# Block-causal attention with a gated linear unit: w_out loaded to all 128 partitions, and a new written order of the work

## The chip, the cores and the metric

The kernel runs on one core of a Trainium2 chip. A core has five engines, each with its own queue of instructions that it runs in order: TensorE (PE: matrix products, with weight loads, PEld, beside them), VectorE (DVE), ScalarE (ACT), GpSimd (POOL) and SyncE (SP, which here issues nearly all transfers). Sixteen DMA engines move the data. The engines wait for each other and for transfers through semaphores. The metric is the time of one execution in microseconds (us).

## The reference

All values are 32 bit floating point. B = 8 batches, H = 8 heads, S = 576 positions, D = 64.

```python
# attention, block-causal in blocks of 64
scores = (1/sqrt(64)) * q @ k^T               # per batch and head, 576 x 576
scores = where(pos_i // 64 >= pos_j // 64, scores, -1e9)
attn = softmax(scores)
x = (attn @ v), heads side by side            # (8, 576, 512)
# gated linear unit with a causal convolution of 5 taps
gate = sigmoid(sum_k conv_w[k] * x shifted by (4 - k) positions)
val = x @ w_val                               # 512 x 512
out = (gate * val) @ w_out                    # 512 x 512
```

## The kernel before

**The work and its names.** The kernel's text holds one long list of words, PLAN; `run` reads it from left to right and calls, for each word, the function that issues that piece of work. Since each engine runs its own instructions in order, the list fixes the order on every engine, and the order of transfers on SP. Nothing else schedules. A word is a name, its indices, and after @ an engine (A = ACT, D = DVE, P = POOL) or the PSUM banks that it uses.

A number Q from 0 to 15 stands for four heads of one batch (Q = 2 x batch + half). For each Q:

- `Lk.Q`, `Lq.Q` load k and q of four heads (576 KB each, line 178) into one of three buffers `qks`.
- `cq.Q.i` casts them to 16 bit (`qk`, line 172, i = 0 for q and 1 for k; the first pair is cast in two pieces), `T.Q.i` transposes on DVE (line 235).
- `s.Q.t` makes score tiles t = 0, 1, 2 on PE; `e.Q.t.a` takes the exponential on ACT (line 269, written into `pt`); `m.Q.t` zeroes the masked corner on POOL (line 285). `sl.b` and `el.b.a` are the last 64 positions of a batch.
- `av.Q.a` multiplies with v, 30 products for two heads; the ones column of v gives the sum, and `n.Q.a` divides by it on DVE (lines 316 and 317) into one of four buffers `x`.

v comes per batch b: `Lv.b.c` loads 128 positions of all heads (256 KB, line 187), c = 0 to 3, `cv.b.0` casts chunks 0 and 1, `cv.b.1` chunks 2 and 3, on POOL. `Lvt.b` and `cvt.b` are the last 64 positions. An `av` of batch b needs all of them.

Then x has to be turned: `xtr.p` (p = 2Q + a, 0 to 31) does it with five products on PE (line 324), followed by a copy `xt.p` out of PSUM on DVE or ACT; or `dx.p` does it as a transposing transfer from SP (line 333), without PE. Before: 13 of the first sort and 19 of the second.

The gated unit works on ten units n: 0 to 7 are the first 512 positions of each batch, 8 and 9 gather the last 64 positions of four batches each (`tt.b` copies them on POOL, line 338). `cn.n` is the convolution (80 small products), `th.n` the gate on ACT (line 366), `val.n.x` the product with w_val (four matrix products), `gv.n.x` gate times value on DVE (line 384), `o.n.t` the product with w_out (four matrix products), `oc.n.t` the copy out of PSUM, `st.n.t` the store (line 416).

**The weights.** w_val comes in two loads (`Lwv`, line 196), and w_out in four (`Lwo.0` to `Lwo.3`, line 201), into buffers `th` that the gates use later. `wo.f@engine` casts half of w_out to 16 bit: f = 0 the columns 0 and 1 of the buffer, f = 1 the columns 2 and 3. Before, `Lwo.j` fills all four columns of 32 partitions, so each `wo` needs all four loads. `w@bank` are products of zeros that keep PE busy while it has nothing to do at the start.

**The first transfers.** `START` issues `Lk.0 Lq.0`; then come the words of PLAN. DVE also builds the convolution's diagonal weights at the start (`cT`, `DG`, lines 428 and 433).

Of the kernel before, what the change touches and what calls it, by code (L numbers as in the profile page):

```python
# [19 lines left out]
el.0.1 s.1.0@0123 e.1.1.1 av.0.0@67 cq.2.1@P e.1.0.0 n.0.0 e.1.0.1 s.1.2@0145 m.1.1 cq.2.0@P T.2.1  # L20
av.0.1@67 e.1.2.1 xtr.0@2 e.1.2.0 m.1.0 T.2.0 cq.3.1@P xt.0@A n.0.1 w@3 w@3 w@3 s.2.1@0145 m.1.2
cq.3.0@P av.1.1@23 e.2.1.0 T.3.1 Lq.4 Lwv.0 e.2.1.1 s.2.2@0167 n.1.1 Lv.1.3 e.2.2.1 av.1.0@45 m.2.1
Lv.1.2 T.3.0 e.2.2.0 s.2.0@2367 n.1.0 cv.1.0@P e.2.0.1 xtr.3@0 xtr.1@1 xt.3@D xtr.2@4 e.2.0.0 m.2.2
xt.1@D xt.2@D w@5 sl.1@0167 cq.4.0@P s.3.0@2345 el.1.1 Lvt.1 el.1.0 e.3.0.0 cn.0@0167 Lk.4 tt.0
wv.0@D Lwo.1 wv.2@P T.4.0 e.3.0.1 Lq.5 val.0.0@2 Lwo.0 wv.3@A wv.1@D Lwo.3 m.2.0 m.3.0 Lk.5
val.0.1@3 th.0.0 cv.1.1@P Lwo.2 Lv.3.1 th.0.1 s.3.2@0145 gv.0.0 Lv.2.0 cvt.1@P gv.0.1 e.3.2.1
av.2.0@67 cq.4.1@P e.3.2.0 av.2.1@23 n.2.0 s.3.1@0145 m.3.2 n.2.1 xtr.4@6 e.3.1.0 val.0.3@7 cq.5.0@P
T.4.1 e.3.1.1 xtr.5@2 val.0.2@3 gv.0.3 xt.4@A m.3.1 xt.5@D s.4.1@0145 gv.0.2 av.3.1@67 e.4.1.1 T.5.0
cq.5.1@P Lv.2.1 e.4.1.0 s.4.2@2345 n.3.1 e.4.2.1 av.3.0@01 Lq.6 wo.0@D wo.1@P Lk.7 e.4.2.0 T.5.1
Lvt.2 s.4.0@4567 Lk.6 m.4.1 n.3.0 xtr.7@2 Lv.2.2 m.4.2 e.4.0.1 o.0.3@3 Lv.2.3 e.4.0.0 xt.7@D  # L30
sl.2@0167 oc.0.3@D cv.2.0@P o.0.1@2 el.2.0 el.2.1 xtr.6@3 m.4.0 oc.0.1@A s.5.2@0145 xt.6@D cq.6.0@P
cn.1@2367 e.5.2.1 e.5.2.0 tt.1 T.6.0 val.1.2@4 cq.7.1@P th.1.1 o.0.2@5 th.1.0 m.5.2 Lv.4.0 gv.1.2
cvt.2@P s.5.0@0167 T.7.1 oc.0.2@A cq.6.1@P val.1.0@4 Lv.3.0 e.5.0.0 val.1.1@5 gv.1.0 e.5.0.1 Lq.7
T.6.1 s.5.1@0123 Lk.8 cv.2.1@P val.1.3@4 Lv.3.3 e.5.1.0 gv.1.1 st.0.3 m.5.0 av.4.0@67 Lk.9 e.5.1.1
gv.1.3 Lv.4.3 s.6.1@0145 n.4.0 m.5.1 cv.3.0@P av.5.0@23 e.6.1.0 xtr.8@6 e.6.1.1 n.5.0 o.1.3@7
cq.7.0@P xt.8@A s.6.2@0145 oc.1.3@D st.0.1 xtr.10@2 m.6.1 e.6.2.0 T.7.0 Lvt.3 o.1.2@3 cq.8.1@P Lvt.4
xt.10@A s.6.0@0167 oc.1.2@D e.6.2.1 o.1.1@2 T.8.1 e.6.0.0 m.6.2 av.5.1@45 oc.1.1@D Lv.5.1 e.6.0.1
av.4.1@01 n.5.1 cq.9.1@P s.7.2@2367 n.4.1 Lq.8 o.1.0@4 e.7.2.0 m.6.0 st.0.2 Lv.4.2 xtr.9@5 e.7.2.1
oc.1.0@D s.7.1@0123 cvt.3@P Lv.3.2 xt.9@D xtr.11@4 cvt.4@P e.7.1.1 o.0.0@5 xt.11@D m.7.2 tt.2
e.7.1.0 sl.3@2367 oc.0.0@D el.3.1 T.9.1 s.7.0@0145 m.7.1 el.3.0 cn.2@2367 e.7.0.0 Lq.9 cq.8.0@P  # L40
Lv.4.1 e.7.0.1 val.2.0@0 Lk.10 T.8.0 th.2.0 Lv.5.0 m.7.0 cv.4.1@P val.2.2@1 th.2.1 gv.2.0 s.8.1@2345
cv.3.1@P val.2.3@0 gv.2.2 e.8.1.1 Lq.11 av.7.0@67 st.1.3 e.8.1.0 gv.2.3 cq.9.0@P st.1.2 s.8.2@0145
Lq.10 n.7.0 Lv.5.3 av.6.1@23 e.8.2.1 cv.4.0@P T.9.0 av.6.0@67 e.8.2.0 m.8.1 Lk.11 n.6.1 cq.10.1@P
dx.14 sl.4@0145 n.6.0 el.4.0 el.4.1 m.8.2 s.9.2@0123 val.2.1@4 T.10.1 e.9.2.0 dx.12 av.7.1@67
cq.11.0@P e.9.2.1 gv.2.1 s.8.0@0145 n.7.1 cv.5.0@P o.2.0@2 e.8.0.1 T.11.0 m.9.2 o.2.2@3 e.8.0.0
dx.15 cq.10.0@P oc.2.0@D s.9.1@4567 Lk.13 oc.2.2@A xtr.13@0 e.9.1.1 o.2.1@1 xt.13@D m.8.0 T.10.0
e.9.1.0 s.9.0@2367 Lv.6.2 oc.2.1@D e.9.0.0 cq.11.1@P av.8.1@45 e.9.0.1 Lv.5.2 s.10.0@0123 n.8.1
m.9.1 e.10.0.0 av.8.0@67 m.9.0 T.11.1 e.10.0.1 s.10.1@0145 tt.3 n.8.0 e.10.1.1 av.9.1@23 m.10.0
dx.17 e.10.1.0 st.2.0 cq.13.1@P cn.3@4567 n.9.1 st.1.1 st.1.0 st.2.1 m.10.1 val.3.3@0 Lq.12 th.3.1
# [44 lines left out]
def kernel(  # L94
# [16 lines left out]
    B, H, SEQ, D = q.shape  # L111
# [24 lines left out]
    DG = const([128, 20, 32], fp16, "DG")  # L136
# [16 lines left out]
    ths = ring(NTH, [128, 4, 512], fp32, "th")  # L153
# [14 lines left out]
    def eng(e, dflt):  # L168
        return ENG[e] if e else dflt
# [340 lines left out]
```

## Time and profile before

| what | value |
|---|---|
| median of 3 runs | 185.18 us (183.21, 185.18, 188.44) |
| the profiled execution's own time | 183.79 us |
| its span, first to last instruction | 182.0 us |
| granted TensorE clock | 0.98 |
| PE busy | 160.2 us (88%) |
| ACT busy | 130.0 us (71%) |
| DVE busy | 116.4 us (64%) |
| POOL busy | 86.8 us (48%) |
| bytes moved by transfers | 43.41 MB |

The span is 1.79 us shorter than the execution's time. Busy times of PE are modelled and include overlap of pipelined products, so that a busy PE is not one at its peak. A transfer's time in the profile runs from its issue on SP to its landing, with the waiting behind earlier transfers in it.

### The profile page before, as it was taken

Reading aid. Unit: us, or ns where it says so; the run is one execution under the profiler, and the core shown is the slowest. Engines: PE = TensorE matmul, PEld = TensorE weight load, DVE = VectorE, ACT = ScalarE, POOL = GpSimd, SP = SyncE. Lnnn points to the kernel's source line nnn. Section 1 sums busy time; section 2 is a strip of 40 time slices with the busy share of each in tenths; the row PEclk is TensorE's granted clock in tenths of the full one; section 3 lists DMA queues with packets and bytes.
Section 4 is the critical chain, followed back from the end, with each engine's and each line's share of the span. In section 5 each row is a group of like instructions: output and inputs, shape, how many; then the busy total and the mean of one; then the engine's idle time right before and its main releaser. Section 6 shows DMA issues by size and latency. Waiting matters only on the chain.

```text
span 182.0 us, 6859 instructions
## 1 busy us (share of the span) xinstructions
PE 160.2 (88%) x2938; PEld 93.0 (51%) x2938; DVE 116.4 (64%) x188; ACT 130.0 (71%) x160; POOL 86.8 (48%) x147
## 2 busy tenths in 40 slices
PE   7796989878798998898998996899999996999991
PEld 2434665636353764485474453655534754755540
DVE  7970897574747798589685438982646874455510
ACT  3499799883789698886995776697899564044461
POOL 6167979542788656877654156645237201000000
PEclk9999699996999999999999999999999999999999
DMA  5999999999999999999999999999999485553155
GB/s 199 370 165 337 383 284 254 266 197 173 247 285 226 305 344 215 303 300 368 205 229 188 385 317 270 296 173 171 222 290 342 136 151 162 107 94 112 69 212 191
DMA packets 61368, 43.41 MB, mean 239 GB/s; under 512 B 51477, under 2 KB 51733, under 8 KB 61338
## 3 DMA queue, kind: packets, MB, share of 16 engines
q1 hardware_dynamic: 61184, 42.84, 96.2%
q8 instruction: 23, 0.38, 0.9%
q10 hardware_dynamic: 154, 0.14, 0.2%
q14 instruction: 7, 0.06, 0.1%
HBM read 30.42 MB, written 9.44 MB: 219 GB/s over the span
## 4 chain that ended last, share of the span: by engine, by line
PE 30%; DMA 28%; SPq 20%; issue 7%; POOL 6%; DVE 4%; ACT 4%; POOLq 0%; DVEq 0%
PE PS L115 29%; DMA qks<-in_k_dram 15%; SPq L187 7%; DMA qks<-in_q_dram 7%; DMA vst<-in_v_dram 5%; SPq L178 4%; SPq L416 3%; POOL qk L172 3%; ACT pt L269 3%; SPq L192 3%; DMA xt<-x 2%; DVE qkT L235 2%; SPq L333 2%; DVE gv L384 1%; POOL w_out L172 1%
## 5 line engine op out<-in xcount | busy, mean ns | idle before, releaser
L269 ACT ACTIVATE pt<-PS 128x1024 f16<-128x1024 f32 x96 | 92.4, 1029 | 22.8 <-PE PS L115 20.1
L172 POOL CAST qk<-qks 128x1152 f16<-128x1152 f32 x30 | 44.6, 1487 | 32.3 <-DMA qks<-in_q_dram 16.5
L235 DVE STREAM_TRANSPOSE qkT<-qk 128x576 f32<-128x576 f32 (+2 forms) x34 | 39.3, 1164 | 12.8 <-POOL qk L172 12.5
L115 PE MATMUL PS<-qkT 32*128 32x64 f16 (+4 forms) x768 | 34.5, 280 | 7.8 <-DVE x L317 2.1
L115 PEld LDWEIGHTS <-pt 128*128 128x128 f16 x960 | 33.9, 100 | 13.5 <-issue 6.2
L115 PE MATMUL PS<-v,pt 128*128 128x65 f16 x896 | 35.8, 198 | 5.7 <-POOL pt L285 2.3
L384 DVE SCALAR_TENSOR_TENSOR gv<-th,PS 128x512 f16<-128x512 f32 (+1 forms) x40 | 26.4, 694 | 16.4 <-ACT th L366 11.5
L115 PE MATMUL PS<-w_out,gv 128*128 128x512 f16 x144 | 34.9, 380 | 0.6 <-POOL w_out L172 0.3
L115 PE MATMUL PS<-xt,w_val 128*128 128x512 f16 x128 | 31.6, 380 | 1.3 <-DMA xt<-x 1.2
L115 PEld LDWEIGHTS <-qkT 32*128 32x128 f16 x768 | 15.7, 94 | 26.6 <-issue 18.6
L366 ACT ACTIVATE th<-PS 128x1024 f32<-128x1024 f32 (+1 forms) x20 | 17.7, 942 | 14.2 <-PE PS L115 14.1
L317 DVE TENSOR_TENSOR x<-PS,rc 128x640 f16<-128x640 f32 x32 | 26.4, 825 | 1.2
L115 PEld LDWEIGHTS <-w_val 128*128 128x128 f16 x160 | 14.2, 97 | 14.7 <-issue 3.4
L115 PEld LDWEIGHTS <-gv 128*128 128x128 f16 x144 | 12.9, 98 | 16.3 <-issue 3.6
L172 POOL CAST v<-vst 128x1024 f16<-128x1024 f32 x16 | 16.6, 1044 | 9.0 <-DMA vst<-in_v_dram 7.9
L285 POOL MEMSET pt<- 64x128 f32 x64 | 11.5, 199 | 15.3 <-ACT pt L269 12.9
L316 DVE RECIPROCAL rc<-PS 128x10 f32<-128x10 f32 x32 | 6.6, 206 | 15.5 <-PE PS L115 13.5
L172 DVE COPY osb<-PS 128x512 f32<-128x512 f32 x17 | 11.5, 682 | 6.2 <-PE PS L115 3.4
L172 ACT COPY osb<-PS 128x512 f32<-128x512 f32 x18 | 10.6, 589 | 4.6 <-PE PS L115 4.4
L115 PE MATMUL PS<-v16t,pt 128*128 128x65 f16 x64 | 12.6, 197 | 0.0
L115 PEld LDWEIGHTS <-DG 32*32 32x32 f16 x800 | 9.0, 88 | 5.3 <-issue 4.0
L115 PE MATMUL PS<-xt,DG 32*32 32x512 f16 x640 | 11.2, 377 | 0.0
(44 smaller groups left out, 71.7 us busy)
## 6 DMA issues: line engine op xcount, KB each, us to landing
qks<-in_k_dram SPq DMA_DIRECT2D x16, 576.0 KB, 6.7
qks<-in_q_dram SPq DMA_DIRECT2D x16, 576.0 KB, 6.4
out_dram<-osb SPq DMA_DIRECT2D x35, 256.0 KB, 4.6
vst<-in_v_dram SPq DMA_DIRECT2D x32, 256.0 KB, 7.1
vtst<-in_v_dram SPq DMA_DIRECT2D x8, 128.0 KB, 6.9
th<-in_moe_w_val_dram SPq DMA_DIRECT2D x2, 512.0 KB, 8.5
th<-in_moe_w_out_dram SPq DMA_DIRECT2D x4, 256.0 KB, 10.4
xt<-x SPq DMA_TRANSPOSE x19, 4.4
```

The source lines that it names most:

```text
L115: nc.tensor.matmul(out=out, lhsT=lhsT, rhs=rhs, start=start, stop=stop, skip_group_check=True)
L172: (e.copy if e is nc.scalar else e.tensor_copy)(out=o, in_=i)
L178: eng(m, nc.sync).dma_start(out=qks[Q % NQS][0:128, i], in_=rows)
L187: eng(m, nc.sync).dma_start(out=vst[b % NVS][0:128, c], in_=v[b, 0:8, 128 * c:128 * c + 128].rearrange("h p d -> p h d"))
L192: eng(m, nc.sync).dma_start(out=vtst[b % 2][0:64, 0:8, 0:64], in_=v[b, 0:8, 512:576].rearrange("h s d -> s h d"))
L235: nc.vector.transpose(out=qkT[Q % NQT][0:128, i].bitcast(fp32)[:, :, 0:288] .rearrange("p a (i n) -> p n a i", n=9)[:, n], in_=qk16[Q % NQ ...
L269: nc.scalar.activation(out=prob(Q, t)[0:128, 2 * a:2 * a + 2, 0:512], in_=PS[0:128, k0:k0 + 2], func=AF.Exp, bias=0.0, scale=0.125)
L285: nc.gpsimd.memset(prob(Q, t)[64:128, 0:4, o:o + 64].bitcast(fp32), 0.0)
L316: nc.vector.reciprocal(out=rc[0:128], in_=O[:, :, :, 64:65])
L317: nc.vector.tensor_tensor(out=x16[p % NX16][0:128].rearrange("p i h d -> p h i d"), in0=O[:, :, :, 0:64], in1=rc[0:128].to_broadcast([128, ...
L366: nc.scalar.activation(out=ths[UO.index(n) % NTH][0:128, 2 * r:2 * r + 2, 0:w], in_=PS[0:128, k0:k0 + 2, 0:w], func=AF.Tanh, bias=0.0, sca ...
L384: nc.vector.scalar_tensor_tensor(out=o, in0=t, scalar=1.0, in1=u, op0=ALU.add, op1=ALU.mult)
```

## The change

Two things change. The first is the load of w_out. A row of w_out has the number 128 x a + 32 x b + i, with a and b from 0 to 3 and i from 0 to 31. Before, load number a took all rows of one a; now load number b takes all rows of one b, for a = 0 to 3 and i = 0 to 31 in this order, and writes them to all 128 partitions, column b of the buffer. Each load still moves 128 rows of 2 KB, and each row ends where it ended before. So a cast `wo.0` needs `Lwo.0` and `Lwo.1` only, `wo.1` the other two.

The second is PLAN: another order of nearly all words and other banks, with the same work except for the following. Four more x tiles are turned on PE and four fewer by a transposing transfer (17 and 15); their copies are five on ACT and twelve on DVE (four and nine before). There is one zero product less (32). The casts of weights go to other engines: `wo.0` on POOL and `wo.1` on ACT (DVE and POOL before), three of the four `wv` on DVE and one on POOL (two on DVE, one each on POOL and ACT before). One piece of the first cast of q goes to POOL instead of DVE, and one copy of an output from ACT to DVE.

```diff
     def load_w_out(j, m):
         eng(m, nc.sync).dma_start(
-            out=ths[1][32 * j:32 * j + 32],
-            in_=moe_w_out[128 * j:128 * j + 128].rearrange("(x i) n -> i x n", x=4))
+            out=ths[1][0:128, j],
+            in_=moe_w_out.rearrange("(j x i) n -> x j i n", j=4, x=4)[j])
```

The order of the transfers on SP up to the loads of w_out, of batch 3's v and of the last q and k (the other words between them left out; "..." marks left out transfers):

```diff
-Lcw Lk.1 Lq.1 Lv.0.1 Lvt.0 Lv.0.0 Lv.0.2 Lv.0.3 Lk.2 Lq.2 Lk.3 Lq.3 Lwv.1 Lv.1.1 Lv.1.0 Lq.4 Lwv.0
-Lv.1.3 Lv.1.2 Lvt.1 Lk.4 Lwo.1 Lq.5 Lwo.0 Lwo.3 Lk.5 Lwo.2 Lv.3.1 Lv.2.0 Lv.2.1 Lq.6 Lk.7 Lvt.2 Lk.6
-Lv.2.2 Lv.2.3 Lv.4.0 Lv.3.0 Lq.7 Lk.8 Lv.3.3 st.0.3 Lk.9 Lv.4.3 st.0.1 Lvt.3 Lvt.4 Lv.5.1 Lq.8 st.0.2
-Lv.4.2 Lv.3.2
...
-dx.22 dx.23 dx.20 Lv.7.2 Lv.6.1 st.3.2 st.3.1 st.8.0 Lq.15 st.3.3 Lk.15 st.3.0 Lvt.6
+Lcw Lq.1 Lk.2 Lk.1 Lq.2 Lv.0.0 Lv.0.2 Lv.0.3 Lvt.0 Lv.0.1 Lk.4 Lq.3 Lk.3 Lq.4 Lk.5 Lv.1.0 Lv.1.1
+Lwv.1 Lwv.0 Lv.1.2 Lv.1.3 Lvt.1 Lwo.0 Lq.5 Lwo.3 Lv.2.2 Lv.2.0 Lwo.1 Lwo.2 Lq.7 Lk.8 Lk.6 Lq.6 Lk.7
+Lv.2.3 Lv.2.1 Lvt.2 Lv.3.0 Lq.8 Lv.3.2 st.0.1 Lv.3.1 Lvt.3 Lvt.4 Lk.9 Lk.10 Lv.4.1 Lv.3.3
...
+dx.16 st.8.0 st.3.0 Lvt.6 st.8.1 dx.18 Lv.6.0 dx.19 st.3.2 st.2.0 Lv.6.1 Lv.7.1 Lk.15 Lq.15 Lvt.7
```

The order on PE around the first use of batch 3's v and from the first use of batch 6's v to the end (banks left out):

```diff
-s.7.0 cn.2 val.2.0 val.2.2 s.8.1 val.2.3 av.7.0 s.8.2 av.6.1 av.6.0 sl.4 s.9.2 val.2.1 av.7.1
...
-av.12.1 s.15.2 av.12.0 o.5.3 av.13.0 sl.7 av.13.1 s.15.1 o.5.1 o.5.0 s.15.0 av.14.1 av.14.0 val.6.3
-av.15.1 av.15.0 val.6.1 cn.6 val.6.0 val.6.2 o.5.2 val.7.1 val.9.0 val.9.3 cn.9 o.6.3 o.6.0 val.9.2
-val.9.1 val.7.2 cn.7 o.6.2 val.7.3 val.7.0 o.9.0 o.6.1 o.7.0 o.7.3 o.7.2 o.7.1 o.9.1
+s.7.2 av.5.0 s.6.0 xtr.11 xtr.10 sl.3 o.1.2 s.8.0 av.7.1 av.7.0 av.6.0 s.8.1 xtr.14 val.2.2
...
+av.12.0 s.13.0 o.4.2 val.5.1 cn.5 val.5.3 val.5.0 val.5.2 sl.7 av.12.1 s.13.2 o.5.0 o.5.1 s.15.0 o.4.0
+av.13.0 s.15.1 av.13.1 s.15.2 o.5.3 s.14.2 o.5.2 av.15.0 av.15.1 av.14.1 av.14.0 val.6.3 val.6.0 xtr.28
+cn.6 val.6.1 val.6.2 val.7.2 val.9.2 val.9.0 cn.9 o.6.3 val.9.1 val.9.3 o.6.0 cn.7 val.7.3 val.7.0
+val.7.1 o.6.2 o.9.0 o.6.1 o.7.1 o.7.2 o.7.3 o.7.0 o.9.1
```

The head of the list, where DVE's `DG` (1.90 us) moves ahead of the transposes `T.0.0`:

```diff
-w@7 cw@0 T.0.1.1 T.0.1.0 cq.0.0.0@A cq.0.0.1@D cT T.0.0.1 T.0.0.0 cq.1.1@P DG w@4 w@4 w@4 w@4 w@4
+w@7 w@7 cw@0 T.0.1.1 T.0.1.0 cT DG cq.0.0.0@A cq.0.0.1@P T.0.0.1 cq.1.0@P T.0.0.0 w@4 w@4 w@4 w@4
```

More of the change, by code (lines that the diff above doesn't have):

```diff
@@ L20 @@
[L20 to L25, printed above, removed]
@@ new lines @@
+xtr.28@0 cn.6@4567 xt.28@A val.6.1@0 th.6.0 val.6.2@1 th.6.1 gv.6.0 tt.7 val.7.2@4 gv.6.1 gv.6.3
+val.9.2@0 gv.6.2 val.9.0@5 cn.9@2367 o.6.3@1 th.9.0 th.9.1 gv.9.0 val.9.1@2 oc.6.3@A val.9.3@3
+gv.9.2 o.6.0@5 st.6.3 gv.9.1 gv.9.3 cn.7@0167 oc.6.0@A st.6.0 val.7.3@5 th.7.0 val.7.0@2 th.7.1
+val.7.1@3 gv.7.0 gv.7.2 o.6.2@0 gv.7.1 o.9.0@1 oc.6.2@A gv.7.3 o.6.1@4 st.6.2 oc.9.0@A o.7.1@0
+st.9.0 oc.6.1@A o.7.2@1 st.6.1 oc.7.1@A o.7.3@2 st.7.1 oc.7.2@A o.7.0@0 st.7.2 oc.7.3@A o.9.1@1
+st.7.3 oc.7.0@A st.7.0 oc.9.1@D st.9.1
```

110 lines of the change are left out of this document (55 added, 55 removed).

## The prediction

> **What bounds the kernel now.** The page comes first: busy shares, the slices, the transfer queue, the chain that ended last.
>
> ```profile
> span 182.0 us, 6859 instructions
> ...
> PE 160.2 (88%) x2938; PEld 93.0 (51%) x2938; DVE 116.4 (64%) x188; ACT 130.0 (71%) x160; POOL 86.8 (48%) x147
> ...
> DMA  5999999999999999999999999999999485553155
> ...
> q1 hardware_dynamic: 61184, 42.84, 96.2%
> ...
> PE 30%; DMA 28%; SPq 20%; issue 7%; POOL 6%; DVE 4%; ACT 4%; POOLq 0%; DVEq 0%
> ```
>
> PE is the busiest engine, but the transfers are full from the second slice to about 140 us, and half of the chain is DMA and SP's queue. The waits, asked for POOL alone (who waited for what: us in total, times, longest), show the hand-over: POOL casts what the loads bring and stands still for them.
>
> ```profile
> POOL qk L172 <- DMA qks<-in_q_dram: 16.5, 14, 3.7
> ...
> POOL qk L172 <- DMA qks<-in_k_dram: 15.0, 9, 4.2
> ...
> POOL v L172 <- DMA vst<-in_v_dram: 7.9, 9, 2.1
> ```
>
> So the stream of loads sets the pace until the last q, k and v are in; then PE works off the rest. Where is the stream slow? By stretches (from:to, length, busy times, then granted clock, DMA share, GB/s):
>
> ```profile
> 14.00:28.00 14.00, 11.85 (x240) 8.35 (x239) 8.93 (x14) 12.60 (x16) 11.00 (x18) 0.88 1.07 338
> 46.00:140.00 94.00, 85.80 (x1662) 48.52 (x1655) 64.48 (x96) 76.94 (x94) 55.21 (x84) 1.00 1.13 271
> ```
> ```profile
> 35.40:46.10 10.70, 8.84 (x160) 6.11 (x156) 6.71 (x10) 6.43 (x8) 4.69 (x6) 0.84 1.12 191
> ```
>
> From 35.4 to 46.1 us, when the w_out loads land, only 191 GB/s move, with all DMA engines busy; the rest of the stream runs at 271, the w_val stretch at 338. In this stretch ACT is busy for 6.43 of 10.7 us. The landings of the four w_out loads and the chain there:
>
> ```profile
> DMA to landing us min/median/max: 7.1/10.4/13.9
> ```
> ```profile
> 31.72 13.05 DMA qks<-in_k_dram
> ...
> 46.29 1.58 POOL w_out L172
> ...
> 49.90 8.23 DMA vst<-in_v_dram
> ```
>
> k of Q = 5, queued among them, needs 13.05 us; the median of the k loads is 6.7:
>
> ```profile
> qks<-in_k_dram SPq DMA_DIRECT2D x16, 576.0 KB, 6.7
> ```
>
> **The change, part by part.**
>
> *The w_out loads.* At 191 GB/s, 10.7 us moved 2.04 MB; at 271 this takes 7.5 us, at 338 6.0. If the new loads run like the others, 3.2 to 4.7 us are gained; I take 4.0, between the two rows. But the new source pattern has a leading count of four (a), then 32 rows, then 512 numbers. Do sixteen DMA engines share such a load? One load in the trace has a leading count below 16: the taps, five rows, on ACT's queue, q10. ACT's other transfer is the last store (128 rows).
>
> ```profile
> q10 hardware_dynamic: 154, 0.14, 0.2%
> ```
> ```profile
> q10 hardware_dynamic: 144, 0.13, 18.7%
> ```
>
> The second row is the stretch 179 to 181 us with that store alone: 144 packets, 128 rows and 16 closing marks, one for each engine. The whole span has ten more: five rows and five marks. The load with leading count five used five engines. So I take it that the new loads, of leading count four, use four engines, 32 rows on each, where the old ones (leading count 32) had 8 rows on each of 16. The trace does not show which count decides when there are 128 rows in all; both ends stay in the range. The price of a 2 KB row, from 166 to 172 us, where only three stores move:
>
> ```profile
> q1 hardware_dynamic: 315, 0.58, 25.5%
> ```
>
> 25.5% of 16 engines for 6 us is 24.5 us, over 0.58 MB / 2 KB = 283 rows 86 ns. So a load holds four engines for 32 x 86 ns = 2.75 us, four of them 11.0 us, and every other load needs these four engines too. The old stretch held w_out and the two loads Lq.5 and Lk.5: 10.7 us. In the new way the same takes 11.0 + 2 x 1.74 (576 KB at 338 GB/s) = 14.5 us: **+3.8 us** on the stream, with bounds of -4.7 (sixteen engines, above) and +7.4 (all of it at the pace of 271 in place of 338: 14.5 x 338/271 = 18.1).
>
> The Trainium skill, "DMA: Bandwidth & Descriptors", section "Why a DMA increments its semaphore by 16 and not by 1", says that a transfer uses the largest number of engines up to 16 that divides the slowest dimension of both patterns; by it the new loads, 4 against 128, run on four, and the sum is the one just made. The taps' five marks agree. The same skill speaks for the change in "SBUF — State Buffer", "Door 1": partitions 0 to 31 reach 8 of 16 ports, 189 against 328 GB/s for 1 MiB, an estimated gain of 2.3 us for 1.05 MB; the stretch at 191 GB/s agrees, and the sum by that rule alone is the second rival's.
>
> *Casts of w_out.* They change engines: `wo.0` from DVE to POOL, `wo.1` from POOL to ACT. Each now needs two of the loads, yet queued behind `wo.1` on ACT are the exponentials of Q = 5, and behind `wo.0` on POOL the casts of Q = 7: if the loads are late, both stop. Hidden by the same lateness of q, k (they queue behind w_out), so nothing extra; 3.5 us if that cover is gone, the difference of 13.9 and 10.4 above.
>
> *Order of loads.* Up to the last chunk of batch 6's v (`Lv.6.1`), SP issues 30 loads of q and k, 32 of v, 7 tails, 13 stores and 11 transposing transfers before; 30, 31, 7, 17 and 4 after. With 0.59, 0.26, 0.13, 0.26 and 0.16 MB each that is 0.36 MB less, at 271 GB/s **-1.3 us**. Up to the last of q and k it is 1.15 MB less (-4.2 us, the lower bound).
>
> *Start.* DG moves ahead of the transposes of the first q on DVE:
>
> ```profile
> 8.43 1.90 DVE L433 TENSOR_TENSOR DG<-idfold,convT 128x640 f16<-128x640 f16 x1
> ```
>
> The first exponential slips by up to 1.9 us. q and k of Q = 1 and 2 are loaded ahead of v, so ACT then has 18 exponentials without a gap; the loads of Q = 3 and 4 hide the slip. I cost it at 0; 1.9 if ACT, not the stream, leads to 45 us.
>
> *Four more tiles on PE*, five products each:
>
> ```profile
> 61.66 0.45 PE L324 MATMUL PS<-ident,x 128*128 128x128 f16 x5
> 141.15 0.58 PE L115 MATMUL PS<-v,pt 128*128 128x65 f16 x14
> 142.30 0.62 PE L115 MATMUL PS<-qkT 32*128 32x320 f16 x16
> 157.56 1.35 PE L115 MATMUL PS<-xt,DG 32*32 32x512 f16 x80
> 171.81 6.21 PE L115 MATMUL PS<-w_out,gv 128*128 128x512 f16 x28
> ```
>
> 4 x 0.45 = 1.8 us, all but `xtr.28` at times when PE waits for loads. Bounds 0.45 and 1.8. Their copies, one more on ACT and three on DVE, fall on engines busy 71% and 64%.
>
> *Banks.* Other banks can make PE wait for a copy where it did not. No row prices it. The longest wait that PE has now for a `pt`:
>
> ```profile
> PE PS L115 <- POOL pt L285: 2.3, 2, 1.9
> ```
>
> One such wait more or less, 1.9 us either way, are the bounds; I take 0.
>
> *The sum.* The place where stream and PE meet last is batch 6's v. Before, its last chunk and the cast:
>
> ```profile
> 128.08 0.56 SPq L187
> ```
> ```profile
> vst<-in_v_dram SPq DMA_DIRECT2D x2, 256.0 KB, 4.1
> ```
> ```profile
> L172 POOL CAST v<-vst x16: 1038/1043/1052, 14.1 to 132.2; 128x1024 f16<-128x1024 f32 x16
> ```
>
> It lands at 128.1 + 4.1 = 132.2. After: 132.2 + 3.8 - 1.3 = 134.7, and cast at 135.7. From its first use before (`av.12.1`, 141.15) the rest took 182.0 - 141.15 = 40.85 us. After, from `av.12.0`, the list has the same work and eleven words more: cn.5 (1.35), two `o` and four `val` (24 products at 6.21/28 = 0.222, 5.3), three score tiles (3 x 0.62 = 1.9), `xtr.28` (0.45): 9.0 us. So the span ends at 135.7 + 40.85 + 9.0 = 185.6, 3.6 more than now. PE reaches that place in time if it keeps its pace: 141.15 - 9.0 = 132.2, plus 1.35 for three tiles, 133.5. The profiled time becomes 183.79 + 3.6 = 187.4. The profiled run and the three runs (183.21, 183.79, 185.18, 188.44) have their middle at 184.5, so I forecast 184.5 x 185.6/182.0 = **188.1 us**.
>
> **The rivals.**
>
> *All sixteen engines.* The change does what it looks like: 132.2 - 4.0 - 1.3 + 1.04 + 49.85 = 177.8, 184.5 x 177.8/182.0 = **180.2 us**. For it: 191 GB/s against 338, and a load of 128 rows has enough to share. Against: the taps' five marks.
>
> *Four engines, and the stream absorbs it.* The other twelve run ahead with later loads; SP issues up to 13.9 us ahead of a landing. If only the lateness of the four is lost and made good by the 1.15 MB, the span is 182.0 + 3.8 - 4.2 = 181.6, **184.1 us**. Against: SP's lead is limited, and a share of 96.2% leaves nothing to make up with.
>
> *PE stops at `av.7.1`.* The new order takes batch 3's v much earlier on PE.
>
> ```profile
> 84.27 0.59 PE L115 MATMUL PS<-v,pt 128*128 128x65 f16 x14
> ```
> ```profile
> 76.08 2.03 POOL L172 CAST v<-vst 128x1024 f16<-128x1024 f32 x2 [0.16 <-POOL pt L285]
> ```
>
> `av.7.1` starts at 84.27 now. Thirteen words that stood ahead of it stand behind it after, and `s.8.0` the other way: three `av` (at most 3 x 1.15, the step from 141.15 to 142.30 above), cn.2 (1.35), three score tiles less one (1.2), sl.4 (0.3, half a tile), four `val` (16 x 0.222 = 3.6), xtr.8 (0.45), 10.4 us. At its present pace PE would be there at 73.9. The cast of the last chunks ends at 78.1 now; 0.72 MB less is loaded ahead (-2.7), and w_out adds 3.8: 79.2. PE stands for 5.3 us. If nothing later gives this back and the four tiles add 1.35, the span is 182.0 + 5.3 + 1.35 = 188.7, **191.2 us**, slower. It decides where PE's work behind it at 80 us is less than now by over 5 us and stays so; against it, the loads after it have slack of their own.
>
> **How the numbers follow.** Chances: forecast 0.45 (185 to 191.5), sixteen engines 0.17, absorbed 0.18, `av.7.1` 0.20. A measurement of this kernel tells about 2% from no change; around 184.5 to 185.18 that is 181.5 and 188.9. Faster by over 2%: sixteen engines, nearly whole (0.15), and 0.03 of absorbed: 0.18. Slower: 0.17 of the `av.7.1` case and 0.20 of the forecast's own range above 188.9: 0.37. Within: 0.45. The range goes down to the sixteen-engine time and up to 193: the forecast with the upper price of the w_out loads (7.4 in place of 3.8: span 189.2, 191.8 us) and most of the 1.9 us of the banks.
>
> **What would show it.** Right: the w_out rows of SP's queue landing about as late as now or later, a stretch around 37 to 52 us below 230 GB/s, ACT or POOL waiting for `th<-in_moe_w_out_dram`; closing marks that are 48 fewer in q1's packets (four loads, 12 engines less each) besides the 2688 packets of four transposing transfers (640 and 32 each). Wrong: that stretch at 270 GB/s or more, with `av.12.0` starting before 130 us. A PE wait of over 3 us ahead of 80 us for POOL's cast of v is the third rival. The forecast is wrong too if ACT, with the same 130 us of work, leads instead of the stream, which its waits for DMA-fed scores would show.

## The result, and the profile after

| what | before | after |
|---|---|---|
| median | 184.69 us (183.21 to 188.44, 4 runs) | 191.56 us (190.06 to 191.9, 4 runs) |
| ratio of the times, with its 95% interval | 1 | 1.0384 (1.0287 to 1.0481) |
| the profiled execution and its span | 183.79, 182.0 us | 190.06, 188.2 us |
| granted TensorE clock | 0.98 | 0.946 |

The changed kernel is 3.8% slower. All ratios in this document, with their intervals, compare only executions within 1.5% of a kernel's quickest, while the medians are over all its executions, so that a ratio is not the quotient of two medians; the profiled executions of two experiments (leading count 2, and the copies of `o.0` on ACT) are about 2% above their quickest. The page of after, with the lines that answer to those shown of before:

```profile
span 188.2 us, 6891 instructions
...
PE   7985888898139999999987999988989999989991
...
PEclk9999579999756999999996999999999999999999
DMA  6999999944996989899899999999997065511165
...
q1 hardware_dynamic: 58448, 42.18, 83.5%
```

Three things stand out. The packets of SP's queue fell by 61184 - 58448 = 2736, exactly the 2688 of the four transposing transfers and 48 closing marks. The queue's share fell from 96.2% to 83.5%, although nearly the same bytes are moved. And there is a hole: from the ninth slice on the DMA engines do four tenths, then PE does one and three tenths, and the granted clock falls to five to seven tenths. A slice is 4.7 us, so this is 38 to 61 us. Two stretches of it and the main one (from:to, length, busy times of PE, PEld, DVE, ACT, POOL, then granted clock, DMA share, GB/s):

```profile
39.00:45.00 6.00, 6.00 (x160) 4.84 (x156) 5.11 (x9) 5.27 (x7) 2.03 (x4) 1.00 0.45 108
45.00:60.00 15.00, 7.25 (x65) 3.29 (x62) 3.17 (x7) 5.49 (x7) 6.09 (x8) 0.66 0.87 256
46.00:140.00 94.00, 81.24 (x1534) 46.26 (x1526) 61.84 (x91) 69.59 (x86) 53.96 (x79) 0.93 1.02 262
```

First the transfers run dry (108 GB/s), then PE does (7.25 us busy of 15, and at 0.66 of the clock). What everybody waits for then, by the waits of after (us in total, times, longest), is w_out:

```profile
ACT w_out L172 <- DMA th<-in_moe_w_out_dram: 8.9, 1, 8.9
...
POOL w_out L172 <- DMA th<-in_moe_w_out_dram: 7.1, 1, 7.1
...
PE PS L115 <- POOL w_out L172: 4.7, 1, 4.7
...
PE PS L115 <- ACT w_out L172: 3.1, 1, 3.1
```

The chain that ended last runs through the same place (start, us, what):

```profile
39.15 4.43 SPq L201
...
43.63 10.30 DMA th<-in_moe_w_out_dram
...
54.00 1.05 ACT w_out L172
...
55.10 1.01 PE PS L115 x2
```

SP's queue is occupied for 4.43 us in issuing the third w_out load; the last one is issued behind it at 43.63 and lands at 53.9; ACT casts; the product `o.0.1` goes on. What comes behind w_out in the queue is late as well. The cast of q of Q = 7 on POOL, in after:

```profile
55.23 2.89 POOL L172 CAST qk<-qks 128x1152 f16<-128x1152 f32 x2 [3.86 <-DMA qks<-in_q_dram]
```

### The profile page after: what moved, and what is told of

It is laid out like the page before. It is cut to its first block, busy times and chain, and to the rows that moved or that the text cites. A ratio compares the mean times of both kernels' runs of the same rounds, so it can differ in the third digit from the quotient of the medians.

```text
span 188.2 us, 6891 instructions
## 1 busy us (share of the span) xinstructions
PE 163.3 (87%) x2957; PEld 94.5 (50%) x2957; DVE 118.5 (63%) x191; ACT 130.2 (69%) x160; POOL 86.6 (46%) x148
## 3 DMA queue, kind: packets, MB, share of 16 engines
q1 hardware_dynamic: 58448, 42.18, 83.5%
## 4 chain that ended last, share of the span: by engine, by line
PE 51%; DMA 18%; ACT 11%; SPq 6%; DVE 5%; issue 4%; POOL 3%; DVEq 0%; POOLq 0%; ACTq 0%
PE PS L115 49%; ACT pt L269 9%; DMA th<-in_moe_w_out_dram 5%; DMA vst<-in_v_dram 4%; DMA qks<-in_q_dram 3%; SPq L187 3%; DMA xt<-x 2%; SPq L201 2%; DMA qks<-in_k_dram 2%; DVE x L317 2%; PE PS L324 2%; DVE qkT L235 1%; POOL v L172 1%; SPq L416 1%; POOL v16t L172 1%
## 5 line engine op out<-in xcount | busy, mean ns | idle before, releaser
L172 POOL CAST qk<-qks 128x1152 f16<-128x1152 f32 (+1 forms) x31 | 45.1, 1470 | 19.5 <-DMA qks<-in_q_dram 16.2
L115 PE MATMUL PS<-w_out,gv 128*128 128x512 f16 x144 | 37.5, 395 | 8.0 <-POOL w_out L172 4.7
L235 DVE STREAM_TRANSPOSE qkT<-qk 128x576 f32<-128x576 f32 (+2 forms) x34 | 38.3, 1163 | 5.3 <-POOL qk L172 4.0
L115 PEld LDWEIGHTS <-pt 128*128 128x128 f16 x960 | 33.2, 100 | 8.5 <-issue 6.0
L115 PE MATMUL PS<-v,pt 128*128 128x65 f16 x896 | 34.4, 197 | 2.9 <-ACT pt L269 1.5
L172 DVE COPY osb<-PS 128x512 f32<-128x512 f32 x18 | 12.4, 688 | 18.7 <-PE PS L115 15.9
L172 ACT COPY osb<-PS 128x512 f32<-128x512 f32 x17 | 10.0, 589 | 5.8 <-PE PS L115 5.8
```

The lines of the kernel that those rows point to most:

```text
L115: nc.tensor.matmul(out=out, lhsT=lhsT, rhs=rhs, start=start, stop=stop, skip_group_check=True)
L172: (e.copy if e is nc.scalar else e.tensor_copy)(out=o, in_=i)
L235: nc.vector.transpose(out=qkT[Q % NQT][0:128, i].bitcast(fp32)[:, :, 0:288] .rearrange("p a (i n) -> p n a i", n=9)[:, n], in_=qk16[Q % NQ ...
```

## The experiments

All ratios are to the kernel before on the same chip. Its medians there were 182.2 us for the first four kernels (new order with sixteen engines, new order with the old load, and the two in the old order), 182.33 for leading count 8, the first late use and the two with sixteen loads, 181.81 for leading count 2, the second late use and the zeros, and 183.72 for the copies on ACT. As the traces come from different chips, small differences in time between them are not read. With leading counts 16, 8 and 2 the rows of w_out arrive in another order, so that these kernels' output is not the reference's; the bytes, the casts and the work are the same. Two questions were open: does the loss come from the load or from the new order, and is it paid because the transfers are late or because PE, ACT and POOL stop in an order that has ready work behind the wait?

**The new order with sixteen DMA engines per load.** Only the number in the source pattern differs from the changed kernel.

```diff
-            in_=moe_w_out.rearrange("(j x i) n -> x j i n", j=4, x=4)[j])
+            in_=moe_w_out.rearrange("(j x i) n -> x j i n", j=16, x=4)[j])
```

> The new order with w_out loads whose source pattern has a leading count of 16 (16 x 8 rows) in place of 4 (4 x 32 rows), still 128 rows of 2 KB to all 128 partitions, so the rows of w_out arrive in another order and the output is not the reference's. Theory 'four engines': the four loads hold every engine for 4 x 8 x 86 ns = 2.75 us in place of 11.0 on four; the waits of 7.1 us (POOL) and 8.9 us (ACT) for w_out go, and the time falls by some 8 us to 183.5 (181 to 185.5). Rival 'the new order is to blame': the time stays at 189 to 192.

Measured: 181.85 us, ratio 0.9932 (0.9869 to 0.9995), inside the expected span. Its stretches, the same as above:

```profile
39.00:45.00 6.00, 6.00 (x145) 4.60 (x144) 4.56 (x9) 5.26 (x7) 2.66 (x5) 1.00 1.14 256
```
```profile
45.00:60.00 15.00, 14.77 (x284) 8.19 (x281) 12.45 (x18) 13.95 (x18) 12.86 (x19) 1.00 1.04 307
```

and its cast of q of Q = 7 on POOL:

```profile
46.41 2.90 POOL L172 CAST qk<-qks 128x1152 f16<-128x1152 f32 x2 [0.28 <-DMA qks<-in_q_dram]
```

The hole is gone: 256 GB/s in place of 108, PE 14.77 us busy in place of 7.25, the full clock, and q of Q = 7 is there 8.8 us sooner. The span is 179.9 us, 8.3 less than after. So the hole goes with the four engines of a load. The new order together with loads on sixteen engines and 128 partitions is 0.7% quicker than the kernel before, less than the 2% that a measurement tells apart.

**The new order with the old load** (32 partitions per load, sixteen engines).

```diff
-            out=ths[1][0:128, j],
-            in_=moe_w_out.rearrange("(j x i) n -> x j i n", j=4, x=4)[j])
+            out=ths[1][32 * j:32 * j + 32],
+            in_=moe_w_out[128 * j:128 * j + 128].rearrange("(x i) n -> i x n", x=4))
```

> The new order with the old load of w_out (32 partitions, leading count 32). Four engines: the loads hold the stream for about 7.5 us (10.7 us less the 3.2 of Lq.5 and Lk.5 there) and each cast needs all four, so a part of the stall stays: 186 to 189. Order to blame: 189 to 192.

Measured: 183.23 us, ratio 1.0116 (1.0035 to 1.0197), a little quicker than expected even when the 1.4% are allowed for by which this chip's kernel before is quicker than the 184.69 us above (that makes 183.5 to 186.5 of the 186 to 189). The stretch:

```profile
39.00:45.00 6.00, 6.00 (x154) 4.74 (x151) 5.11 (x10) 5.01 (x6) 2.03 (x4) 1.00 1.10 208
```

All engines are busy (1.10), yet only 208 GB/s move against the 256 of sixteen engines on 128 partitions. So loads to 32 partitions do cost something: 1.8% in this order by the ratios, 0.8% by the medians. Part of it can be that each cast here needs all four loads (POOL waits 4.4 us for w_out, ACT 2.1), which was not tried apart. Loads on four engines cost more: from 1.0116 to the changed kernel's 1.0384 are 2.7%. The remaining 1.2% belong to the new order with the old load, which by itself is slower than the kernel before.

**The old order with the new load, and with the new load on sixteen engines.** The load is exchanged in the kernel before, as shown above; its PLAN stays.

> The old order with the new load (leading count 4). Four engines: 3.8 us more on the stream, more if the waits for the casts add to it: 188 to 192. Order to blame: 183 to 186, as before.

> The old order with the loads of leading count 16 (rows of w_out in another order, output not the reference's). Four engines, and 32 partitions slow in the kernel before: 3.2 to 4.7 us off the stream, 180 to 182. If the 191 GB/s of that stretch had another cause: 184 to 185.

Measured: 186.22 us, ratio 1.0263 (1.02 to 1.0326), for the first. The times expected stood on the slower chip; scaled to this one they are 185.5 to 189.4, and the result lies inside. For the second a median of 182.12 us of four runs (178.7 to 184.85), which can't be told from the 182.2 of the kernel before: the expected gain (scaled, 177.6 to 179.6) was missed. The old order with the new load from 37 to 52 us:

```profile
37.00:52.00 15.00, 8.03 (x139) 4.84 (x131) 8.75 (x14) 8.18 (x9) 4.79 (x8) 0.87 0.54 154
```

The same hole in another order: 154 GB/s, DMA share 0.54, PE 8 of 15 us, where the kernel before has 223 GB/s, 1.10 and 12 us. The exchange of the load costs about as much here, 2.6%, as in the new order. In the old order the sixteen engines bring no gain that these runs show.

**The dose.** If engines = leading count and 86 ns a row is the price, then 8 and 2 have to give half and twice the load's time.

```diff
-            in_=moe_w_out.rearrange("(j x i) n -> x j i n", j=4, x=4)[j])
+            in_=moe_w_out.rearrange("(j x i) n -> x j i n", j=8, x=4)[j])
```

> The changed kernel with w_out read with leading count 8 (8 x 16 rows per load; which rows a load takes is changed, so the output is not the reference's; bytes, casts and order are the same). Theory A (engines = leading count, 86 ns a row): a load holds 8 engines for 16 x 86 ns = 1.4 us, the four 5.5 us where leading count 4 took 11.0 and 16 took 2.75: the closing marks on SP's queue are 32 more than in the changed kernel, and the time lies between, ratio 1.00 to 1.015. Rival (a threshold: anything below sixteen engines is as bad as four): ratio 1.03 or more.

> The changed kernel with w_out read with leading count 2 (2 x 64 rows per load; which rows a load takes is changed, so the output is not the reference's). Theory (engines = leading count, 86 ns a row): 64 x 86 ns = 5.5 us per load on two engines, 22.0 us for the four where leading count 4 took 11.0: closing marks 8 fewer on SP's queue than in the changed kernel, w_out later by 8 to 11 us, ratio 1.08 to 1.11 to the kernel before. Rival (the price does not go by engines times rows): anything below 1.06.

Measured: 184.18 and 200.47 us, ratios 1.0134 (0.9945 to 1.0323) and 1.1025 (1.0875 to 1.1175), both inside what the first theory expected, though the interval of the first is wide. The packets of SP's queue with leading counts 16, 8 and 2:

```profile
q1 hardware_dynamic: 58496, 42.18, 87.6%
```
```profile
q1 hardware_dynamic: 58464, 42.18, 86.5%
```
```profile
q1 hardware_dynamic: 58440, 42.18, 78.8%
```

Four loads with 12 marks more, 4 more and 2 fewer than after's four give +48, +16 and -8 to 58448, and so it is. (The expectation for eight named 32 more: it counted eight added marks a load, where there are four.) The stretch 39 to 45 us and the cast of q of Q = 7 with leading count 8:

```profile
39.00:45.00 6.00, 6.00 (x116) 3.64 (x114) 4.24 (x8) 5.06 (x6) 2.36 (x5) 1.00 0.83 171
```
```profile
49.79 2.90 POOL L172 CAST qk<-qks 128x1152 f16<-128x1152 f32 x2 [1.85 <-DMA qks<-in_q_dram]
```

and with 2:

```profile
39.00:45.00 6.00, 6.00 (x102) 3.60 (x100) 3.92 (x7) 5.06 (x7) 2.82 (x4) 1.00 0.32 92
```
```profile
65.25 2.87 POOL L172 CAST qk<-qks 128x1152 f16<-128x1152 f32 x2 [7.11 <-DMA qks<-in_q_dram]
```

| leading count | engines x rows | four loads at 86 ns a row | q of Q = 7 cast from | DMA share, GB/s at 39 to 45 us | ratio |
|---|---|---|---|---|---|
| 16 | 16 x 8 | 2.75 us | 46.41 us | 1.14, 256 | 0.9932 |
| 8 | 8 x 16 | 5.5 us | 49.79 us | 0.83, 171 | 1.0134 |
| 4 (the change) | 4 x 32 | 11.0 us | 55.23 us | 0.45, 108 | 1.0384 |
| 2 | 2 x 64 | 22.0 us | 65.25 us | 0.32, 92 | 1.1025 |

Against sixteen engines the price grows by 2.75, 8.25 and 19.25 us, the cast comes 3.4, 8.8 and 18.8 us later. So the q that is queued behind these loads is late by the time that they hold their few engines, and by little else.

**Is it the stop in the order?** PE stands before `o.0.1` with scores of Q = 5 ready behind it, ACT before `wo.1` with exponentials behind it. In a first try the casts and `o.0` move some 30 words later.

```diff
-gv.0.2 wo.0@P xtr.5@0 e.4.2.0 n.3.0 av.3.1@67 wo.1@A xt.5@D m.4.2 xtr.6@1 n.3.1 s.5.1@2345 xt.6@A o.0.1@0
-cq.7.0@P e.5.1.1 xtr.7@1 oc.0.1@D e.5.1.0 s.5.2@4567 xt.7@D cq.8.1@P o.0.3@0 e.5.2.0 o.0.0@1 e.5.2.1
-oc.0.3@D tt.1 cq.6.1@P sl.2@2345 oc.0.0@D o.0.2@0 el.2.0 el.2.1 T.7.0 s.5.0@2345 m.5.2 oc.0.2@A
-Lvt.2 cq.6.0@P T.6.1 e.5.0.0 Lv.3.0 cn.1@0167 T.8.1 e.5.0.1
+gv.0.2 xtr.5@0 e.4.2.0 n.3.0 av.3.1@67 xt.5@D m.4.2 xtr.6@1 n.3.1 s.5.1@2345 xt.6@A
+cq.7.0@P e.5.1.1 xtr.7@1 e.5.1.0 s.5.2@4567 xt.7@D cq.8.1@P e.5.2.0 e.5.2.1
+tt.1 cq.6.1@P sl.2@2345 el.2.0 el.2.1 T.7.0 s.5.0@2345 m.5.2
+Lvt.2 cq.6.0@P T.6.1 e.5.0.0 Lv.3.0 e.5.0.1 wo.0@P wo.1@A o.0.1@0 oc.0.1@D o.0.3@1
+oc.0.3@D o.0.0@0 oc.0.0@D o.0.2@1 oc.0.2@A cn.1@0167 T.8.1
```

> The changed kernel, loads of w_out with leading count 4 as they are, but the two casts of w_out and the four products o.0 behind them moved some 30 words later on their engines, to just ahead of cn.1, so that the scores and exponentials of Q = 5 no longer stand behind them. Theory A (the loss is the stop of PE, ACT and POOL in their orders, which lets 8 exponentials and 4 score tiles wait that were ready): about 5 of the 6.2 us come back, ratio 1.00 to 1.015 to the kernel before. Rival B (the loss is in the stream; what comes later waits for q and k of Q = 6 and 7 that are as late as now): ratio 1.03 to 1.045, with the waits for w_out replaced by waits of POOL for q and k of the same length.

Measured: 197.11 us, ratio 1.0935 (1.0857 to 1.1014), outside both. The waits of this kernel say why:

```profile
PE PS L115 <- POOL w_out L172: 11.5, 1, 11.5
```

`wo.0` was moved past four casts of q and k of Q = 6 to 8 on POOL, which come later than w_out, and PE waited 11.5 us in place of 4.7. The try says nothing on the question. In the second, both casts stand on POOL at the old place of `wo.0`, and only `o.0` and its copies are moved.

```diff
-gv.0.2 wo.0@P xtr.5@0 e.4.2.0 n.3.0 av.3.1@67 wo.1@A xt.5@D m.4.2 xtr.6@1 n.3.1 s.5.1@2345 xt.6@A o.0.1@0
+gv.0.2 wo.0@P wo.1@P xtr.5@0 e.4.2.0 n.3.0 av.3.1@67 xt.5@D m.4.2 xtr.6@1 n.3.1 s.5.1@2345 xt.6@A
...
+Lvt.2 cq.6.0@P T.6.1 e.5.0.0 Lv.3.0 e.5.0.1 o.0.1@0 oc.0.1@D o.0.3@1
+oc.0.3@D o.0.0@0 oc.0.0@D o.0.2@1 oc.0.2@A cn.1@0167 T.8.1
```

> The changed kernel, loads of w_out with leading count 4 as they are; both casts of w_out now stand on POOL, at the place of the first (ahead of the casts of q and k of Q = 7, 8 and 6, which come later than w_out anyway), and only the products o.0 and their copies are moved later, to just ahead of cn.1. So on PE and ACT nothing that is ready stands behind w_out. Theory A (the loss is that PE and ACT stop in their orders with scores and exponentials of Q = 5 ready): the exponentials go on from 45 to 53 us in place of stopping until 55.5, the next stop is where q of Q = 7 lands, and about 5 of the 6.2 us come back: ratio 1.00 to 1.015 to the kernel before. Rival B (the loss is in the stream, q and k of Q = 6 to 8 are what PE lacks): PE stops as long at the scores of Q = 6 to 8 instead, ratio 1.025 to 1.045.

Measured: 193.95 us, ratio 1.0738 (1.063 to 1.0846), again outside both. ACT and PE of this kernel:

```profile
46.94 3.77 ACT L269 ACTIVATE pt<-PS 128x1024 f16<-128x1024 f32 x4
50.58 0.69 ACT L279 ACTIVATE pt<-PS 128x256 f16<-128x256 f32 x2
51.76 1.94 ACT L269 ACTIVATE pt<-PS 128x1024 f16<-128x1024 f32 x2 [0.50 <-PE PS L115]
```
```profile
54.17 2.72 PE L115 MATMUL PS<-w_out,gv 128*128 128x512 f16 x6 [1.71 <-POOL w_out L172]
61.00 3.57 PE L115 MATMUL PS<-w_out,gv 128*128 128x512 f16 x8 [4.12 <-DVE osb L172]
```

The ready work did run, from 46 to 53 us. But then PE's next word was `o.0`, and its copies stood on DVE behind the transposes of Q = 6 and 7, whose q and k had not come: 4.12 us. Without that fault, the copies on ACT:

```diff
-e.5.0.1 o.0.1@0 oc.0.1@D o.0.3@1 oc.0.3@D o.0.0@0 oc.0.0@D o.0.2@1 oc.0.2@A cn.1@0167
+e.5.0.1 o.0.1@0 oc.0.1@A o.0.3@1 oc.0.3@A o.0.0@0 oc.0.0@A o.0.2@1 oc.0.2@A cn.1@0167
```

> The changed kernel with both casts of w_out on POOL and o.0 moved later as before, but now the four copies of o.0 stand on ACT, which idles there, and no longer on DVE behind the transposes of Q = 6 and 7, for which PE waited 4.12 us. So this is the test of an order without that fault. Theory A (the loss is the stop of PE and ACT with ready work behind it): ratio 1.00 to 1.02. Theory B (the loads behind w_out are late by some 8.8 us, the casts of q and k of Q = 7 start at 55 us in place of 46.4 with sixteen engines, and no order on PE makes that good): PE's stop moves to where it needs Q = 6 to 8, batch 6's last v is cast at 133 to 136 us as in the changed kernel, ratio 1.03 to 1.05.

Measured: 189.75 us, ratio 1.0518 (1.0415 to 1.0621). This is no better than the changed kernel. PE of this kernel, which stands from 52.7 to 56.3 us:

```profile
51.87 0.85 PE L115 MATMUL PS<-w_out,gv 128*128 128x512 f16 x2
56.30 6.13 PE L115 MATMUL PS<-w_out,gv 128*128 128x512 f16 x14 [3.59 <-POOL w_out L172]
```

The scores and exponentials ran first, and no time was won, so the first theory, that the stop in the order is the loss, is not borne out. The ratio lies a little above the second's 1.03 to 1.05, its interval reaches into them. The test is not a clean one: behind `o.0` still stand `cn.1` and four `val`, which need neither w_out nor the late q and k, and `cn.1` starts at 62.4 us, as in the changed kernel (62.3). What the order is worth is better seen where PE meets the stream last, below.

**Is it the halved clock after the stop?** 38 products of zeros ahead of `o.0.1` keep PE busy while it waits.

```diff
-m.4.2 xtr.6@1 n.3.1 s.5.1@2345 xt.6@A o.0.1@0
+m.4.2 xtr.6@1 n.3.1 s.5.1@2345 xt.6@A
+w@0 w@0 w@0 w@0 w@0 w@0 w@0 w@0 w@0 w@0 w@0 w@0 w@0 w@0 w@0 w@0 w@0 w@0 w@0
+w@0 w@0 w@0 w@0 w@0 w@0 w@0 w@0 w@0 w@0 w@0 w@0 w@0 w@0 w@0 w@0 w@0 w@0 w@0
+o.0.1@0
```

> The changed kernel with 38 products of zeros (128 x 512, some 0.22 us each, 8.2 us) on PE ahead of o.0.1, where PE waits 4.69 and 3.06 us for w_out and the clock granted afterwards is half from 49.3 to 59.6 us. The wait itself ends when it did. Theory (the half clock follows PE's idle stretch and costs what PE does from 55.1 to 59.6 us at half speed, up to 2.2 us): no half clock from 49 to 60 us, ratio 1.02 to 1.03 to the kernel before. Rival (after the stop PE is short of q and k, so its speed there costs nothing): the clock is full but the ratio stays 1.03 to 1.045.

Measured: 189.26 us, ratio 1.0489 (1.0375 to 1.0604), outside the theory's span and a little above the rival's 1.03 to 1.045, which its interval reaches. The clock is full in the stretches that had half of it:

```profile
45.00:52.00 7.00, 7.00 (x69) 3.63 (x66) 1.92 (x4) 0.46 (x1) 1.38 (x3) 1.00 0.99 245
52.00:60.00 8.00, 7.49 (x66) 3.50 (x65) 2.37 (x5) 5.61 (x8) 4.44 (x4) 1.00 0.84 266
```

and no time is won. Where the gain went is seen at `av.12.0`, the first use of batch 6's v. PE in this kernel, then in the changed one:

```profile
137.16 0.32 PE L117 MATMUL PS<-v,pt 128*128 128x65 f16 x5
139.43 0.47 PE L117 MATMUL PS<-v,pt 128*128 128x65 f16 x9 [1.96 <-POOL pt L287]
```
```profile
139.04 0.32 PE L115 MATMUL PS<-v,pt 128*128 128x65 f16 x5
139.87 0.47 PE L115 MATMUL PS<-v,pt 128*128 128x65 f16 x9 [0.52 <-POOL pt L285]
```

With the full clock PE is there 1.88 us sooner, but its next nine products wait for a mask on POOL and start only 0.44 us sooner. The mask stands on POOL behind the casts of the last q and k, and these stand behind their loads. The last cast of q of this kernel, of the changed one, and of the new order with sixteen engines:

```profile
137.11 1.47 POOL L174 CAST qk<-qks 128x1152 f16<-128x1152 f32 x1 [0.56 <-DMA qks<-in_q_dram]
```
```profile
137.54 1.49 POOL L172 CAST qk<-qks 128x1152 f16<-128x1152 f32 x1 [0.24 <-DMA qks<-in_q_dram]
```
```profile
129.80 1.48 POOL L172 CAST qk<-qks 128x1152 f16<-128x1152 f32 x1 [0.35 <-DMA qks<-in_q_dram]
```

The zeros leave it nearly where it was; sixteen engines bring it 7.7 us sooner. What PE wins on its own in between is given back at the mask; besides, from 140 to 146 us the granted clock of the kernel with the zeros is 0.72, against 1.00 in the changed one. The same place in the kernels of the new order (us; "goes on" is the start of the last nine products of `av.12.0`, each time after a wait for the mask):

| kernel | `av.12.0` starts | last cast of q starts | `av.12.0` goes on | span |
|---|---|---|---|---|
| leading count 16 | 130.07 | 129.80 | 132.13 | 179.9 |
| leading count 8 | 131.66 | 131.35 | 133.68 | 181.6 |
| old load | 133.61 | 132.72 | 135.06 | 182.9 |
| leading count 4 (the change) | 139.04 | 137.54 | 139.87 | 188.2 |
| the same, with zeros | 137.16 | 137.11 | 139.43 | 188.8 |
| the same, `o.0` late, copies on ACT | 137.72 | 138.29 | 140.60 | 190.2 |
| leading count 2 | 148.70 | 148.63 | 150.94 | 199.3 |

In every row PE goes on 2.3 us after the last cast of q starts, whenever it came there itself, and 48 to 50 us later the kernel ends. So the time follows the last q. Why it is late is seen in the bytes: from 39 to 60 us the changed kernel moved 108 x 6 + 256 x 15 = 4490 KB, with sixteen engines 256 x 6 + 307 x 15 = 6140 KB. From 46 to 140 us both move 262 GB/s, with shares of 1.02 and 1.03, so that nothing is made up: 1.65 MB less is at this rate an estimated 6.3 us, of the 7.7. The kernels with the zeros and with the copies on ACT moved no more than the changed one by then (4.5 and 4.4 MB). The full stream carries most of the 8.8 us of the start to its end. Stops of the engines can add to that: in the first two kernels with the later use the loads are the same, but from 60 to 130 us the DMA share is 0.88 and 0.97, against 1.01 in the changed kernel, and the last cast of q starts at 144.87 and 140.55.

**Sixteen loads of 64 KB**, so that each is shared by sixteen engines and each row still ends where it must.

```diff
+        for x in range(4):
+            eng(m, nc.sync).dma_start(
+                out=ths[1][32 * x:32 * x + 32, j],
+                in_=moe_w_out[128 * x + 32 * j:128 * x + 32 * j + 32])
```

> The changed kernel with each w_out load cut into four: sixteen loads of 32 consecutive rows (64 KB), each to 32 partitions of one column, so that every row ends where it did and the casts need the same columns. Theory A (what cost was that four DMA engines carried a load): each of these loads is shared by sixteen engines, 2 rows each, so the time is that of the new order with leading count 16, ratio 0.99 to 1.00 to the kernel before on the same chip, no wait for w_out over 1.5 us, 37 to 52 us above 290 GB/s. Rival B (what a load needs is all 128 partitions at once; 32 at a time are slow however many engines carry them): like the new order with the old load, ratio 1.01 to 1.02 and 280 GB/s or less. Rival C (twelve more transfers on SP's queue cost in themselves, by some 0.1 us of issue each and more of start): 1.2 us or more above A.

> The kernel before, order unchanged, with the same sixteen loads of 32 rows. Theory A: like the old order with leading count 16, whose profiled execution took 178.7 us: ratio 0.975 to 0.995, waits for w_out below 1 us in place of the kernel before's. Rival B: no change, ratio 0.995 to 1.005.

Measured: 184.52 us, ratio 1.0201 (1.0105 to 1.0297), in the new order, and 183.02 us, ratio 0.9985 (0.9895 to 1.0075), in the old one. SP's queue and a stretch of the first:

```profile
37.78 6.63 SPq L202 DMA_DIRECT2D th<-in_moe_w_out_dram  x8
```
```profile
40.00:45.00 5.00, 5.00 (x127) 3.84 (x124) 4.11 (x9) 4.26 (x6) 2.37 (x5) 1.00 0.34 103
```

SP needs 6.63 us for eight of these small loads: 0.42 us, the median of the sixteen, for each of the last six, but 2.25 and 1.55 for the first two, for which the trace names no cause. Behind them the transfers run dry, 103 GB/s with a DMA share of 0.34, as with four engines, but for another reason: here each load has its sixteen closing marks (58688 packets, 240 more than after's) and no engine is held; the next loads are not issued. The second theory's numbers would fit as well (1.01 to 1.02, and 220 GB/s from 37 to 52 us), but by it the engines would be busy, as with the old load (1.10). So this is the third of the theories, the price of issue, at 0.42 us and more a load in place of the expected 0.1. Against four loads on sixteen engines it comes to 2.7% by the ratios, whose intervals are about 1% to either side, and to 2.2 us by the spans (182.1 and 179.9). In the old order the ratio is in the span of the second theory; whether it is also the price of issue that takes a gain away there was not told apart. None of these kernels is quicker than the kernel before by more than a measurement tells apart.

## Why the prediction was right or wrong

The time, 191.56, lies in the range and 1.8% above the forecast of 188.1; the forecast said 1.95% over its base of 184.5, the runs say 3.8%. What the loads do was foreseen rightly; the loss was put at half, and the place where it becomes time was not the one named. The range held the result because it went up to 193 for other reasons (the upper price of the loads, the banks), and so far that is luck.

*Four engines per load:* right, shown by the 48 marks and by the counts of 2, 8 and 16. The Trainium skill, "DMA: Bandwidth & Descriptors", section "Why a DMA increments its semaphore by 16 and not by 1", has the rule that the slowest dimension decides; the closing marks of all four counts agree. *The price, 86 ns a row:* right, the dose agrees with it.

*Load and order.* The sum put +3.8 us (2.1%) on the load and, with -1.3 us for the transfers and all else, nearly nothing on the order: without the +3.8 it ends at 132.2 - 1.3 + 1.04 + 49.85 = 181.8, against 182.0 before. Measured, the load costs 2.6% in the old order and 2.7% in the new one, some 4.8 us, and the new order with the old load costs 1.2%, some 2 us. So by these ratios the order's part was missed by more than the load's. What in the new order costs this was not tried; in it POOL, ACT and PE wait 4.4, 2.1 and 2.0 us for w_out.

*The gain of all 128 partitions* (-4.0 us as a rival): too large for the time, not for the stream (below). In the new order the step from the old load to sixteen engines on 128 partitions is 1.8% by the ratios, from 1.0116 to 0.9932; in the old order none is seen. The sixteen-engine rival's 180.2 us was 2.3% below its base; the kernel that does this is 0.7% below. By the figures of the Trainium skill's "SBUF — State Buffer", "Door 1", the estimate for the loads alone was 2.3 us. The 1.8%, of 182.2 us, are 3.3 us, of the same size, but only in this order, and with the casts' need of all four loads in it. (The prediction gave the sum by that rule to the second rival; it is the first one's.)

*The stream, +3.8 - 1.3 us:* about right. The last chunk of batch 6's v was to be cast by 135.7 us with four engines and by 132.2 - 4.0 - 1.3 + 1.04 = 127.9 with sixteen. POOL in after, then with sixteen engines:

```profile
132.00 2.03 POOL L172 CAST v<-vst 128x1024 f16<-128x1024 f32 x2 [0.23 <-DMA vst<-in_v_dram]
```
```profile
125.32 2.03 POOL L172 CAST v<-vst 128x1024 f16<-128x1024 f32 x2 [2.05 <-DMA vst<-in_v_dram]
```

That is 134.0 and 127.4.

*"The place where stream and PE meet last is batch 6's v":* **this step failed.** `av.12.0` needs more than v: in the new list the mask `m.12.2`, which it reads, stands on POOL behind the casts of the last k and q. So its last products start not at 135.7 but at 139.87, 5.8 us after its v is cast, and with sixteen engines they wait for the same mask:

```profile
132.13 0.47 PE L115 MATMUL PS<-v,pt 128*128 128x65 f16 x9 [1.74 <-POOL pt L285]
```

The table above shows this place in seven kernels of the new order. The sum had the numbers for it. The last cast of q and k before is

```profile
139.11 1.48 POOL L172 CAST qk<-qks 128x1152 f16<-128x1152 f32 x1 [0.30 <-DMA qks<-in_k_dram]
```

so it ends at 140.6, and with the prediction's own +3.8 and -4.2 us up to there at 140.2 after; measured are 139.0.

*"PE reaches that place in time if it keeps its pace: ... 133.5":* this step failed too, but it did not set the time. `av.12.0` starts at 139.04 in after (the row above); with sixteen engines PE starts it at

```profile
130.07 0.32 PE L115 MATMUL PS<-v,pt 128*128 128x65 f16 x5
```

9.0 us sooner. PE did not keep its pace in after: it did 7.25 us of work from 45 to 60 us in place of 14.77, as it stood 4.7 and 3.1 us for w_out and had half the clock behind that. The sum charged the lateness of the loads only where v ends. But where PE came 1.88 us sooner, in the kernel with the zeros, its work went on only 0.44 us sooner.

*Casts of w_out, "hidden by the same lateness of q, k, so nothing extra":* the waits are there, 8.9 us on ACT and 7.1 on POOL, and PE waited 4.7 and 3.1 us behind them. That they cost nothing beside the lateness of the stream agrees with the kernels that let the ready work run and were not quicker; as none of these is free of another stop, it is not shown.

*The rest behind `av.12.0`:* put at 49.85 us, measured 188.2 - 139.87 = 48.3 from where it goes on (with sixteen engines 179.9 - 132.13 = 47.8). So the span of 188.2 in place of 185.6 is 4.2 us later at this place and 1.5 us less behind it. *Four tiles, banks, start:* not measured one by one.

*The rivals.* The `av.7.1` case gave 191.2, nearest to the result, but by another mechanism. In after it starts at 80.88 us with no wait:

```profile
80.88 0.60 PE L115 MATMUL PS<-v,pt 128*128 128x65 f16 x14
```

So a time that fits does not speak for its story. "The stream absorbs it" is refuted: against sixteen engines the last q is 7.7 us late.

## What to carry to other kernels

Before a load's pattern is changed, count the leading dimension: here the loads with four there were slower (1.0384) than the ones to a quarter of the partitions with 32 there (1.0116), and they delayed what was queued behind them for as long as they held their few engines. To find where a full stream sets the time, look for the last thing that an engine waits for, with what stands in the queues between: here not the last v, but a mask behind the casts of the last q and k. Cutting a transfer into many to reach all engines has its own price in the issuing queue, here 0.42 us a load.

## What the runs showed that was not expected

- Twelve idle DMA engines did not run ahead with the loads behind. The share at 39 to 45 us was 0.45 with four engines and 0.32 with two, and SP's queue stood 4.43 us in the issue of one w_out load, so that q of Q = 7 was issued only at 44.3 us. With sixteen engines one such issue took 3.12 us too, but there the share was 1.14. Why an issue takes so long the trace does not say, and a second queue was not tried.
- Small loads are not cheap to issue: sixteen of 64 KB took SP's queue 0.42 us each in the median, about as long as the four of 256 KB before (0.43 to 0.66), and while it issued the last of them the DMA engines were at a share of 0.34.
- The granted clock was half for some 10 us after PE's stop (49.3 to 59.6 us in after), was full when zeros filled the stop, and no time was won by it (1.0489 against 1.0384, the intervals overlap).
